# Sixteen expert slots with 3264 columns in place of 3287

## The chip, the core and the metric

The kernel runs on one core of one Trainium2 chip. The metric is the device time of one execution in microseconds (us). The kernel before took 423.11 us, the median of 6 runs that lay between 422.43 and 423.81 us.

A core has five engines that run side by side and wait for each other through semaphores: TensorE (PE; its weight loads are a row of their own, PEld), VectorE (DVE), ScalarE (ACT), GpSimd (POOL) and SyncE (SP), which here issues most of the DMAs. Matmul results land in PSUM and are copied from there by DVE or ACT into SBUF.

## The reference: what is computed

Two blocks, one after the other, in float32.

The first block is a recurrence (rwkv5) over 768 steps for 4 batches and 8 heads of 48 channels. Its output, seen as rows, is `x` with 3072 tokens of 384 values:

```python
cur = np.einsum('bhd,bhe->bhde', u[None] * kt, vt)
y[:, :, t] = np.einsum('bhd,bhde->bhe', rt, state + cur)
state = w[None, :, :, None] * state + np.einsum('bhd,bhe->bhde', kt, vt)
```

The second block sends each token to one expert of 16: to the best of 4 groups, and in that group to the best of 4 experts. Each expert is a two-layer network of 384 to 1024 to 384, and its result is scaled by the product of two softmax weights:

```python
g_idx = np.argmax(x @ w_group, axis=1)            # the group
e_idx = np.argmax(xg @ w_expert[g], axis=1)       # the expert in the group
h = np.maximum(xg[mask_e] @ w1[g, e], 0.0)
ye = h @ w2[g, e]
out[tok_idx] = combined[:, None] * ye
```

## The kernel before, in words

The kernel has two stages. In the first, 24 tiles of 128 tokens go through the recurrence in chunks, are routed, and their rows are scattered to a DRAM buffer `x_sorted`, which has a region for each expert. In the second, the experts are worked off one after the other.

How many tokens an expert gets is only known at run time, but each instruction has a fixed shape. So the kernel sorts the experts by their token counts on the chip and gives them *slots* of falling size. The list `SLOTS` (line 20) holds the sizes. The expert in slot `e` is computed with `SLOTS[e]` token columns, however few tokens it has; the columns that are left hold zeros, or rows whose index lies outside of the output. The first two experts are chosen early, after 16 of the 24 tiles (`pick_first`), the other 14 by the final counts. If an expert has more tokens than its slot (the comparison with `most`, lines 975 to 985 write the result to `left_i`), a slow path under `tc.If(more > 0)` (line 1039 on) handles the tokens that are left over, in further slots of 128 tokens, each with its own load of the weights.

The work of the second stage is a list of 17 items (`ITEMS`): the first slot of 256 is split in two items of 128 columns, and each other slot is an item of its own, of `SLOTS[e]` columns. An item of width w consists of:

- `columns` (L561, DVE): three transposes of the gathered rows `xg` into `xe`. They work on w rounded up to a multiple of 32 (`padded`).
- `up` (L596, PE): the first layer, in four calls (f = 0, 2, 4, 6). Each has 6 matmuls that move w columns, and ACT's ReLU to `hT` follows (L600). In the trace each matmul of float32 appears twice, so the four calls give 48 PE records.
- `w2_part` (L480, ACT): four copies of 128 x 768 that rearrange the second layer's weights; they don't depend on w.
- `down` (L617, PE): the second layer, in three calls (d = 0, 1, 2) of 8 matmuls that move w columns (48 records), each followed by ACT's copy to `yo` (L620).
- `pieces_out` (L649, L651, L656): DVE transposes and scales the result, on the padded width, and POOL scatters it to the output in pieces of 32 tokens. The last item goes another way (`turn_out`, `rows_out`, L634, L636, L669).

The order on PE and DVE is written out by hand (`manual_schedule`). For item i PE does `up(i, 0)`, `up(i, 2)`, `down(i-1, 1)`, `up(i, 4)`, `up(i, 6)`, `down(i-1, 2)`, `down(i, 0)`, then item i+1 begins. On DVE `pieces_out(i-1)` stands before `columns(i+1)`, so the transposes that item i+1 needs come after the last output work of item i-1.

Weights lie in two places used in turn: `w` (w1 and w2) and the memory of `kall` and `rall`, which the first stage has left. SP loads those of the expert after next as soon as `up(i, 6)` has read the last of w1 (L484 and L489), and it loads the rows of the item after next (L548, L554). PSUM gives 6 buffers (`bank`) in turn to all of these.

Of the kernel before, what the change touches and what calls it, by code (L numbers as in the profile page):

```python
# [16 lines left out]

SLOTS = [256, 240, 233, 222, 216, 212, 206, 202, 199, 196, 193, 190, 187, 184, 178, 173]  # L20
CAP = max(SLOTS)
FOUR = 4

# [11 lines left out]
def kernel(  # L35
# [30 lines left out]
    assert RING * 2 * H * D == KO * F and RING * 2 * H * DP >= FO * DM  # L66
    assert len(SLOTS) == GE == 16 and all(P < n <= 2 * P for n in SLOTS) and GE * (N + 1) < 2**20 and NCH > FOUR and FOUR * B * P >= GE * P
    assert DM % P == 0 and F % P == 0 and G == Eg == 4 and DM <= 512 and NT * GE <= 512
# [178 lines left out]

    for i, n in enumerate(SLOTS):
        nc.gpsimd.memset(most[:, i : i + 1], float(GE * n + GE - 1) + FIRST * max(2 - i, 0))
# [258 lines left out]

    ITEMS = [(0, 0, P), (0, P, SLOTS[0])] + [(e, 0, SLOTS[e]) for e in range(1, GE)]
    pools = {0: early}  # L510
# [528 lines left out]
    with tc.If(more > 0, preferred_fallthrough_block=False):  # L1039
        with tc.tile_pool(name="rest", bufs=1) as rest:  # L1040
# [7 lines left out]
            room = rest.tile([P, GE], FP32, name="room")  # L1048
            for i, n in enumerate(SLOTS):
                nc.vector.memset(room[:, i : i + 1], float(n))  # L1050
# [216 lines left out]
```

## Time and profile before

One execution was profiled. Its own time was 423.4 us, and the span from its first to its last instruction 421.6 us.

| What | Before |
|---|---|
| Median of 6 runs | 423.11 us |
| Profiled execution: time, span | 423.4 us, 421.6 us |
| PE busy | 406.3 us, 96% of the span |
| PE weight loads busy | 382.1 us, 91% |
| DVE busy | 183.2 us, 43% |
| ACT busy | 215.2 us, 51% |
| POOL busy | 202.2 us, 48% |
| HBM read, written | 70.15 MB, 16.44 MB |
| Granted TensorE clock, mean | 0.998 |

How to read what follows: a line of a profile names the line of the kernel (L617), the engine, the operation, and what it writes and reads (`po<-hT,w_parts`). `128*128 128x240` at a matmul means a stationary operand of 128 by 128 and a moving one of 128 rows by 240 columns. A line of the list in order of time begins with its start and its length in us; `x24` says that 24 instructions in a row were merged. Where an engine had to wait, the line ends in brackets with the length of the wait and what ended it. A line of busy time by stretch has the stretch (start and end in us), its length, and then for each of PE, PEld, DVE, ACT and POOL the busy time and, in brackets, the instructions; behind them stand the granted clock of PE, the busy share of the DMA engines and GB/s. The ends of matmuls are modelled, so that one of a row seems to overlap the next: what a matmul costs in a row of them is read from the starts.

### The profile page before, as it was taken

How to read it: one execution, taken by the hardware profiler on the slowest of the kernel's cores; microseconds unless marked ns; L12 is line 12 of the kernel's file. 1: busy time of each engine (PE TensorE's matmuls, PEld its weight loads, DVE VectorE, ACT ScalarE, POOL GpSimd, SP SyncE). 2: the span in 40 equal slices, each digit the busy share in tenths (PEclk: the TensorE clock that was granted, in tenths of full speed). 3: DMA queues.
4: the chain of work that ended last, by engine and by line, in shares of the span. 5: the costliest groups of instructions: out<-in, count | busy, mean ns of one | idle time of the engine just before them, and what ended most of it. 6: DMA issues, size and time to landing. Idle time of an engine off the chain costs nothing. (4 is left out here: it accounts for less than half of the span.)

```text
span 421.6 us, 9930 instructions
## 1 busy us (share of the span) xinstructions
PE 406.3 (96%) x3649; PEld 382.1 (91%) x3649; DVE 183.2 (43%) x620; ACT 215.2 (51%) x505; POOL 202.2 (48%) x214
## 2 busy tenths in 40 slices
PE   7799999999999989999999999999999999999993
PEld 6678888888887789999999999999999999999993
DVE  6566879787977834122130322304303403312211
ACT  2797777777776403551615426255255155256430
POOL 6875567777770733030624516336236246225453
PEclk9999999999999999999999999999999999999999
DMA  9999999991183959999987989789899899999001
GB/s 172 208 257 282 273 265 213 222 219 45 41 206 108 302 149 265 268 216 249 252 167 210 254 195 270 167 247 280 171 256 271 187 253 261 207 270 263 22 26 36
DMA packets 124476, 86.67 MB, mean 206 GB/s; under 512 B 96998, under 2 KB 113565, under 8 KB 124420
## 3 DMA queue, kind: packets, MB, share of 16 engines
q1 hardware_dynamic: 112732, 69.05, 72.5%
q0 software_dynamic: 4960, 9.48, 7.1%
q10 hardware_dynamic: 6728, 7.44, 5.2%
q8 instruction: 30, 0.49, 0.5%
q14 instruction: 26, 0.21, 0.2%
HBM read 70.15 MB, written 16.44 MB: 205 GB/s over the span
## 5 line engine op out<-in xcount | busy, mean ns | idle before, releaser
L656 POOL DMA_INDIRECT out_dram<-yp,ids x104 | 101.0, 972 | 160.2 <-DVE yo L611 124.7
L617 PE MATMUL po<-hT,w_parts 128*128 128x128 f32 (+15 forms) x816 | 139.4, 327 | 0.0
L617 PEld LDWEIGHTS po<-hT,w_parts 128*128 128x128 f32 x816 | 133.7, 190 | 0.9
L649 DVE STREAM_TRANSPOSE yr<-yo 128x224 f32<-128x224 f32 (+3 forms) x48 | 21.8, 460 | 181.9 <-ACT yo L620 181.3
L600 ACT ACTIVATE hT<-ph 128x256 f32<-128x256 f32 (+15 forms) x68 | 33.5, 492 | 79.8 <-PE ph L596 79.8
L596 PE MATMUL ph<-xe,w 128*128 128x128 f32 (+7 forms) x432 | 71.4, 322 | 1.3 <-DVE xe L561 1.3
L596 PEld LDWEIGHTS ph<-xe,w 128*128 128x128 f32 x432 | 68.5, 191 | 2.0 <-DVE xe L561 1.5
L596 PE MATMUL ph<-xe,kall 128*128 128x240 f32 (+7 forms) x384 | 68.5, 334 | 0.0
L596 PEld LDWEIGHTS ph<-xe,kall 128*128 128x128 f32 x384 | 65.4, 190 | 0.6
L705 ACT ACTIVATE am<-ident,du 128x128 f32<-128x128 f32 x192 | 58.7, 390 | 1.9 <-DVE du L697 1.5
L620 ACT COPY yo<-po 128x128 f32<-128x128 f32 (+15 forms) x51 | 16.2, 323 | 80.9 <-PE po L617 64.8
L735 DVE COPY_PREDICATED am<-later,pa 128x512 f32<-128x512 uint32 x48 | 32.7, 729 | 12.8 <-ACT yT L764 5.6
L480 ACT COPY w_parts<-rall 128x768 f32<-128x768 f32 x32 | 38.0, 1235 | 0.0
L480 ACT COPY w_parts<-w 128x768 f32<-128x768 f32 x29 | 34.4, 1234 | 0.0
L457 POOL DMA_INDIRECT x_sorted<-xt,place_i x24 | 23.8, 992 | 19.4 <-DVE rb L822 13.7
L691 POOL TENSOR_TENSOR dg<-rall,kall 128x768 f32<-128x768 f32 (+1 forms) x13 | 22.1, 1702 | 22.2 <-DVE du L697 21.3
L730 PE MATMUL pa<-rT,kT 48*128 48x128 f32 x384 | 28.8, 285 | 0.1
L758 PE MATMUL py<-am,vt 128*64 128x128 f32 x384 | 26.7, 280 | 0.0
L730 PEld LDWEIGHTS pa<-rT,kT 48*128 48x128 f32 x384 | 23.9, 187 | 2.2 <-issue 0.5
L684 POOL TENSOR_TENSOR kh<-kall,T 128x768 f32<-128x768 f32 (+1 forms) x12 | 21.6, 1804 | 8.5 <-DMA kall<-in_k_dram 5.9
L758 PEld LDWEIGHTS py<-am,vt 128*64 128x64 f32 x384 | 20.4, 136 | 4.7 <-issue 3.7
L720 ACT COPY kT<-pk 128x512 f32<-128x512 f32 x24 | 14.0, 583 | 20.4 <-PE pk L716 18.7
(146 smaller groups left out, 403.7 us busy)
## 6 DMA issues: line engine op xcount, KB each, us to landing
w<-in_moe_w_dram SPq DMA_DIRECT2D x32, 384.0 KB, 6.8
w<-in_moe_w_dram SPq DMA_DIRECT2D x8, 1536.0 KB
kall<-in_moe_w_dram SPq DMA_DIRECT2D x32, 384.0 KB, 8.0
rall<-in_moe_w_dram SPq DMA_DIRECT2D x8, 1536.0 KB, 12.6
x_sorted<-nothing ACTq DMA_DIRECT2D x4, 1544.0 KB, 8.1
rall<-in_r_dram SPq DMA_DIRECT2D x12, 384.0 KB, 7.1
vt<-in_v_dram SPq DMA_DIRECT2D x12, 384.0 KB, 7.2
kall<-in_k_dram SPq DMA_DIRECT2D x10, 384.0 KB, 6.0
```

The lines of the kernel that those rows point to most:

```text
L457: ins = nc.gpsimd.indirect_dma_start(out=xs_dram, out_offset=bass.IndirectOffsetOnAxis(ap=place_i[:, i : i + 1], axis=0), in_=xt[:, i, :], ...
L480: copy(w2_parts[e % 2][:, a : a + 2], w2[:, a : a + 2, :].rearrange("p f (c k) -> p f k c", k=KO))
L596: nc.tensor.matmul(ph[:, q, :], lhsT=w1[:, ko, P * (f + q) : P * (f + q + 1)], rhs=xe[:, ko, 0:w], start=(ko == 0), stop=(ko == KO - 1), s ...
L600: nc.scalar.activation(hTs[i][:, f : f + 2, 0:w], ph, AF.Relu)
L617: nc.tensor.matmul(po, lhsT=w2[:, fo, d, :], rhs=hT[:, fo, 0:w], start=(fo == 0), stop=(fo == FO - 1))
L649: nc.vector.transpose(yr[:, 0:b, :, d], y[:, d, 0:w].rearrange("p (b t) -> p b t", t=BL))
L656: ins = nc.gpsimd.indirect_dma_start(out=out_pieces, out_offset=bass.IndirectOffsetOnAxis(ap=ids[:, j : j + 1], axis=0), in_=yp[:, j], in_ ...
L691: engine.tensor_mul(dg, rts[g % RING][:, a0:a1, :, 0:D], kts[g % RING][:, a0:a1])
L705: nc.scalar.mul(am[:, e, hc, :], ident, dus[n // 2][:, n % 2, h : h + 1])
L730: nc.tensor.matmul(pa[e][:, hc, :], lhsT=kT[rows, hc, :], rhs=rT[rows, hc, :], start=True, stop=True, skip_group_check=True,)
L735: nc.vector.copy_predicated(am[:, e], earlier, pa[e])
L758: nc.tensor.matmul(py[e][DP * o : DP * (o + 1), j, :], lhsT=vt[:, a, 4 * o + 2 * j + e, :], rhs=am[:, e, 2 * o + j, :], start=(c == 0), st ...
```

## The change

The list of slot sizes gets new numbers; nothing else in the program differs. The old sizes add up to 3287 columns, the new ones to 3264.

```diff
-SLOTS = [256, 240, 233, 222, 216, 212, 206, 202, 199, 196, 193, 190, 187, 184, 178, 173]
+SLOTS = [256, 237, 233, 220, 214, 209, 205, 202, 199, 194, 193, 189, 185, 183, 176, 169]
```

Slot by slot the losses are 0, 3, 0, 2, 2, 3, 1, 0, 0, 2, 0, 1, 2, 1, 2 and 4 columns, 23 in all. The largest slot stays at 256 (`CAP`), which sizes the tiles and the zeroed part of each region, so no tile moves in memory. Every slot keeps its padded width (a multiple of 32), so all DMAs, the transposes of DVE and the scatters of POOL keep their shapes, but for the last item's second output tile, which has 41 rows in place of 45. The order of the instructions and their waits is the same on all five engines; what differs are the widths in L596, L600, L617 and L620, in the memsets that fill a result up to its padded width (L611), in the last item's row counts (L570, L574, L634, L636, L669) and the constants of `most`.

## The prediction

> **What bounds the kernel now.** I read the page first: which engine is busy, and where its idle time lies (in a group's line, behind the first bar the busy us and the mean ns of one, behind the second the idle us before them and what ended it).
>
> ```profile
> span 421.6 us, 9930 instructions
> PE 406.3 (96%) x3649; PEld 382.1 (91%) x3649; DVE 183.2 (43%) x620; ACT 215.2 (51%) x505; POOL 202.2 (48%) x214
> L617 PE MATMUL po<-hT,w_parts 128*128 128x128 f32 (+15 forms) x816 | 139.4, 327 | 0.0
> L596 PE MATMUL ph<-xe,w 128*128 128x128 f32 (+7 forms) x432 | 71.4, 322 | 1.3 <-DVE xe L561 1.3
> L596 PE MATMUL ph<-xe,kall 128*128 128x240 f32 (+7 forms) x384 | 68.5, 334 | 0.0
> ```
>
> PE is busy in 96% of the span, and the three groups of expert matmuls, 279 us together, had idle time before them once: 1.3 us at the start of the second stage (157.16 us), where no changed slot has begun. A busy share doesn't say that PE sets the end, so next came PE's waits from 185 us to the end; the answer is one line:
>
> ```profile
> PE pb L634 <- ACT yo L620: 0.4, 1, 0.4
> ```
>
> That is the last output tile. No expert matmul waited for a weight load from DRAM, a row gather, an eviction or a transpose. The busy time by stretch, cut where PE starts one item and the next (columns: PE, PEld, DVE, ACT, POOL), says it again:
>
> ```profile
> 157.16:162.62 5.46, 5.46 (x48) 5.46 (x49) 5.24 (x32) 1.15 (x3) 2.01 (x3) 1.00 0.79 226
> 189.00:406.90 217.90, 217.90 (x1289) 217.22 (x1288) 55.44 (x208) 96.31 (x147) 88.49 (x92) 1.00 0.87 216
> 218.31:235.99 17.68, 17.68 (x98) 17.68 (x97) 4.33 (x19) 7.46 (x11) 7.85 (x9) 1.00 0.86 213
> 365.48:380.52 15.04, 15.04 (x99) 15.04 (x97) 3.83 (x17) 7.17 (x11) 5.79 (x7) 1.00 0.98 251
> 380.52:395.16 14.64, 14.64 (x99) 14.64 (x97) 3.78 (x17) 7.16 (x11) 5.75 (x7) 1.00 0.63 177
> ```
>
> The reader is to see that PE's busy time equals the stretch in each, at full clock (1.00), and that items get shorter with their slots: 216 columns (the third line) take 17.68 us, 178 (the last) 14.64. ACT needs half of an item, DVE a quarter.
>
> **What a column costs.** From the first `up` of one item to that of the next lie 48 records of `up` and 16 of `down(i, 0)` at the item's own width and 32 of `down(i-1, 1)` and `down(i-1, 2)` at that of the item before. The 216 item (before it 222) is 64 x 216 + 32 x 222 = 20928 columns, the 178 item (before it 184) 64 x 178 + 32 x 184 = 17280. So a column costs (17.68 - 14.64) / (20928 - 17280) = 0.833 ns; 20928 x 0.833 ns is 17.44 us, and the other 0.24 us over 96 records are 2.5 ns for each. The 184 item checks it: 64 x 184 + 32 x 187 = 17760 columns, 14.80 + 0.24 = 15.04 us, as the fourth line has it.
>
> **Does it hold for the new widths?** Two ways in which it may not. First, weight loads: if these set the pace, narrower matmuls gain nothing. The first line above has 48 records of 128 columns, 113.8 ns each; whatever the floor is, it is no higher than that, and the narrowest new record, 169 columns, takes 169 x 0.833 + 2.5 = 143.3 ns. Second, odd widths: ten of the new slots are odd, five of the old ones. In order of time:
>
> ```profile
> 334.68 4.02 PE L596 MATMUL ph<-xe,kall 128*128 128x190 f32 x24
> 338.54 2.78 PE L617 MATMUL po<-hT,w_parts 128*128 128x193 f32 x16
> 350.20 3.96 PE L596 MATMUL ph<-xe,w 128*128 128x187 f32 x24
> 354.00 2.74 PE L617 MATMUL po<-hT,w_parts 128*128 128x190 f32 x16
> ```
>
> From start to start 24 records of 190 take 3.86 us and 24 of 187 take 3.80; the rate gives 3.860 and 3.800. An odd width costs nothing that this trace resolves (0.01 us in a run of 24). Five items turn from even to odd (237, 209, 205, 189, 183), each with 2 runs of `up` and 3 of `down`; at 0.01 us for each of these 25 runs it would be 0.25 us at most, in either direction.
>
> A rule is weighed here. The Trainium skill, "TensorE: Matmul & The Clock Gate", section "Back-to-back issue gap", gives for sustained pairs of weight load and matmul about 81 ns at 128 columns and 131 ns at 512, a slope of 0.13 ns a column. By that the saving below would be an estimated 0.29 us, which nobody could measure. Its formula for one matmul alone, N/2.4 + 2.5 ns, has the 2.5 ns of these rows but half their slope, and would give 0.92 us. The rows here are this kernel's own float32 records, and I take them.
>
> **The sum.** Removed: 23 columns (3, 2, 2, 3, 1, 2, 1, 2, 1, 2, 4 in the slots that change), each in 96 records of its item: 23 x 96 x 0.833 ns = 1.84 us, all on PE's gapless path. What else the change moves:
>
> - ACT's ReLUs and copies get shorter by under 1 ns a column (240 columns copied in 358 ns, 173 in 304). They hide beside PE, and what hides them is that ACT is idle for half of each item. ACT's four weight copies keep their length; they end some 4.8 us before `down` reads them (387.9 and 392.7 us in the 178 item).
> - DVE's memsets grow by up to 12 elements at 0.84 ns (78 ns for 24, 136 for 93): 10 ns, beside PE.
> - The tail after the last `down`, from 414.67 us to the end: one copy of 304 ns gets 3 ns shorter, and two DVE and one POOL instruction of 45 rows take 41. DVE's 45 rows took 540 ns against 572 for 128, so I cost this at zero.
> - DMAs keep sizes and order. SP's loads are released by PE (`up(i, 6)`), so they start earlier with it, and each deadline moves up by no more than an item and a half shrinks, 0.5 us. The tightest are those for the 233 item: w1 is issued until 167.0 us and there after at most 9.0, at 176.0, where PE wants it at 180.75; its rows until 161.6, there after at most 13.6, at 175.2, where DVE turns them at 179.1; its w2 at 167.4, and even with the 13.4 us of the longest w2 landing it is there at 180.8, where ACT copies it at 184.0. Later ones have more: for the 184 item, `kall` is issued until 347.2 and there after at most 8.5 us, at 355.7 for a use at 365.3. POOL scatters 6 to 8 pieces at 1.28 us a piece, 10.2 us of at least 14.6.
>
> So nothing is late next by these rows, except perhaps one wait, which is the closest thing in the trace. Before each item DVE writes `xe` only after it has scaled the item before last (`pieces_out(i-1)`), and PE covers this with `down(i, 0)`, which gets shorter, while DVE's padded widths don't:
>
> ```profile
> 393.77 0.76 DVE L651 TENSOR_TENSOR yp<-yr,gates 128x576 f32<-128x576 f32 x1
> 394.50 0.33 DVE L561 STREAM_TRANSPOSE xe<-xg 128x192 f32<-128x192 f32 x1
> 395.01 1.81 PEld L596 LDWEIGHTS ph<-xe,kall 128*128 128x128 f32 x12
> ```
>
> `xe` is there at 394.83 and PE's weight load begins at 395.01: 0.18 us. At no other item is it less. From ACT's last copy to PE's weight load for it took 0.06 us (414.70 + 0.30 to 415.06), so some 0.12 us are free. The change takes from it 16 records times the columns lost by the covering item: 2 columns here, 27 ns; 40 ns at most (3 columns), where 0.3 us are free. I take no wait. If none of this slack were usable, the 16 of 96 records of each item that cover it would gain nothing: 1.84 / 6 = 0.31 us lost. So the gain is 1.53 to 1.84 us for this term, and with the 0.25 us for odd widths 1.28 to 2.09.
>
> The profiled execution took 423.40 us (span 421.6 and 1.8 around it): 423.40 - 1.84 = 421.56. It stood 0.29 us above the median of 423.11, so the median is forecast at 421.27 us, 0.43% lower. About 0.2% (0.85 us) is what a measurement of this kernel can tell from no change; its six runs spread over 1.4 us.
>
> **Rivals.**
>
> 1. *The DVE chain takes it* (`xe` late at each item): 0.31 us lost, 421.6 us; still faster. For it: the slack falls to 0.18 us. Against it: 27 to 40 ns are taken.
> 2. *The experts are bound by data, and PE's lead is given back as waits for weights*: no change, about 423.1 us. For it: the DMA share is 0.86 to 0.99 from item to item. Against it: no PE wait on a DMA after 157 us, and the 3.2 us and more of slack above, which 1.8 us over the whole stage can't use up.
> 3. *A slot is too small* (the other side, slower): one expert with a token more than its slot sends the whole kernel through the slow path at L1039. Counting the reference's routing on its inputs, in slot order, gives 206, 211, 208, 207, 200, 200, 199, 198, 195, 193, 185, 185, 183, 170, 170 and 162 tokens. All fit; the tightest are 193 in 194 and 183 in 185 (before 193 in 196). It decides from two tokens more in that one expert, or three in the other. The nearest two candidates of any token differ by 2.8e-6 where the group logits spread by 0.01, so a rounding on the chip moves hardly one token. Price: a gather (at least 7.6 us), 96 records at 113.8 ns (10.9 us) and a scatter (6.2 us), 25 us at least; with its 16 zeroing stores in a row at 2.3 us, the shortest landing of a gather, and a weight load of 13.4 us, 75 us: 448 to 498 us.
> 4. *The narrower slots do nothing* (a pace set by weight loads): 423.1 us. Against it: 0.833 ns a column holds from 233 down to 173 columns.
>
> **How the numbers follow.** The forecast has 0.88, rival 1 0.06, rivals 2 and 4 together 0.04, rival 3 0.02. Rival 1 is also faster by over 0.2%, so faster has 0.94, same 0.04, slower 0.02. The time is the forecast's, 421.3. The range takes the gain of 1.28 to 2.09 us and 0.3 us more at both ends for where a median of few runs falls (as far as the profiled execution stood from it): 423.11 - 2.09 - 0.3 = 420.7 and 423.11 - 1.28 + 0.3 = 422.1.
>
> **What would show it.** The span falls to 419.75 us and PE's last `down` ends 1.84 us earlier, at 412.83. A stretch like the 216 item's (214 now, 220 before it) takes 64 x 214 + 32 x 220 = 20736 columns, 17.52 us. PE's waits after 185 us stay one line of 0.4 us; `xe` is ready 0.15 us or so ahead of PE at the last item. I am wrong if PE waits for `xe` or a DMA in the second stage, if the columns cost more at odd widths, or if lines of L1046 and later appear.

## The result: slower by 0.27%, and the profile after

The changed kernel took 424.24 us, the median of 17 runs (423.74 to 425.06), against 423.13 us for the kernel before (37 runs, 422.43 to 423.81). The ratio is 1.0027, with a 95% interval of 1.002 to 1.0033. The forecast was 421.3 us.

The profiled execution has a span of 423.1 us, 1.5 us more than before. The first question is whether the columns gave what they should. The busy time by stretch, first of the kernel before and then of the changed one, is cut at three places that both have: PE's first `up` of the second stage, PE's last two transposes, and POOL's last scatter (columns as before: stretch, length, then PE, PEld, DVE, ACT and POOL, the granted clock, the DMA share, GB/s).

```profile
157.16:415.06 257.90, 257.51 (x1540) 255.40 (x1540) 66.04 (x260) 112.50 (x172) 101.04 (x104) 1.00 0.87 214
415.06:417.37 2.31, 0.44 (x2) 0.18 (x2) 0.64 (x2) 0.00 (x0) 0.97 (x2) 1.00 0.04 11
417.37:421.60 4.23, 0.00 (x0) 0.00 (x0) 0.00 (x0) 0.00 (x0) 0.91 (x1) 0.78 0.19 67
```

```profile
157.41:413.47 256.06, 255.67 (x1540) 253.82 (x1541) 66.16 (x260) 112.25 (x172) 101.04 (x104) 1.00 0.87 216
413.47:415.78 2.31, 0.44 (x2) 0.18 (x2) 0.63 (x2) 0.00 (x0) 0.97 (x2) 1.00 0.04 11
415.78:423.10 7.32, 0.00 (x0) 0.00 (x0) 0.00 (x0) 0.00 (x0) 1.42 (x1) 0.63 0.13 39
```

The expert matmuls gained what was forecast: 257.90 - 256.06 = 1.84 us. The next stretch is the same. But from POOL's last scatter to the end it now takes 7.32 us where it took 4.23: 3.09 us more, over the 1.84 us that PE saved. (The second stage also began 0.25 us later. Nothing in the first stage was changed, and I don't explain that; in the profiled executions of the first four experiments below this start lay between 156.06 and 156.73 us, so it moves by more than that from one execution to the next.) The sum, -1.84 + 3.09 + 0.25, is the 1.5 us of the spans.

The last scatter is the one that writes the second output tile of the last item: 45 rows before, 41 now. The two scatters of L669 in order of time, before and after:

```profile
416.09 0.97 POOL L669 DMA_INDIRECT out_dram<-yt,ids  x1 [3.19 <-DVE yt L636]
417.37 0.91 POOL L669 DMA_INDIRECT out_dram<-yt,ids  x1 [0.30 <-POOLq L1039]
```

```profile
414.50 0.97 POOL L669 DMA_INDIRECT out_dram<-yt,ids  x1 [2.95 <-DVE yt L636]
415.78 1.42 POOL L669 DMA_INDIRECT out_dram<-yt,ids  x1 [0.30 <-POOLq L1039]
```

The first writes 128 rows and takes 0.97 us in both. The second has four rows less and takes POOL half a microsecond more. SP's wait for it at the end of the program, and the packets of POOL's DMA queue (the page's list of queues), again before and after:

```profile
SPq L1262 <- DMA out_dram<-yt,ids: 1.5, 1, 1.5
...
q0 software_dynamic: 4960, 9.48, 7.1%
```

```profile
SPq L1262 <- DMA out_dram<-yt,ids: 4.5, 1, 4.5
...
q0 software_dynamic: 5168, 9.48, 7.1%
```

The wait grew by 3.0 us, and the queue carries 208 packets more. That number is the clue. In the trace the rows of a tile leave in packets of up to three rows. 45 rows made 16 packets (besides 16 of 4 bytes, which both kernels have). 41 rows on one DMA engine make 14, and 14 on each of 16 engines are 224, which is 208 more than 16. By their sizes only 12 of the 224 hold rows of the output, and 12 of the 16 before; the others are 8 or 12 bytes long. So it looked as if 45 rows went to 15 engines with 3 rows each, and 41, a prime, to a single engine. The Trainium skill, "DMA: Bandwidth & Descriptors", section "Why a DMA increments its semaphore by 16 and not by 1", has such a rule: the number of engines is the largest up to 16 that divides the slowest dimension on both sides of the transfer. The page also has an exception on trn2, for some direct copies; the scatter here is an indirect one, and the runs have to tell. The experiments were made to see whether it is this that cost the time.

### The profile page after: what moved, and what is told of

Read it like the earlier page. It is cut to its first block, busy times and chain, and to the rows that moved or that the text cites. A ratio compares the mean times of both kernels' runs of the same rounds, so it can differ in the third digit from the quotient of the medians.

```text
span 423.1 us, 9930 instructions
## 1 busy us (share of the span) xinstructions
PE 405.1 (96%) x3649; PEld 381.0 (90%) x3649; DVE 183.3 (43%) x620; ACT 215.0 (51%) x505; POOL 202.5 (48%) x214
## 3 DMA queue, kind: packets, MB, share of 16 engines
q0 software_dynamic: 5168, 9.48, 7.1%
## 5 line engine op out<-in xcount | busy, mean ns | idle before, releaser
L617 PE MATMUL po<-hT,w_parts 128*128 128x128 f32 (+15 forms) x816 | 138.5, 326 | 0.0
L617 PEld LDWEIGHTS po<-hT,w_parts 128*128 128x128 f32 x816 | 133.0, 190 | 0.8
L600 ACT ACTIVATE hT<-ph 128x256 f32<-128x256 f32 (+15 forms) x68 | 33.5, 492 | 78.5 <-PE ph L596 78.5
L596 PE MATMUL ph<-xe,w 128*128 128x128 f32 (+7 forms) x432 | 71.1, 321 | 0.9 <-DVE xe L561 0.9
L596 PEld LDWEIGHTS ph<-xe,w 128*128 128x128 f32 x432 | 68.3, 191 | 1.5 <-DVE xe L561 1.0
L596 PE MATMUL ph<-xe,kall 128*128 128x237 f32 (+7 forms) x384 | 67.9, 333 | 0.0
L596 PEld LDWEIGHTS ph<-xe,kall 128*128 128x128 f32 x384 | 64.9, 190 | 0.5
L620 ACT COPY yo<-po 128x128 f32<-128x128 f32 (+15 forms) x51 | 16.2, 321 | 80.1 <-PE po L617 68.5
```

What stands on the lines that cost most here:

```text
L596: nc.tensor.matmul(ph[:, q, :], lhsT=w1[:, ko, P * (f + q) : P * (f + q + 1)], rhs=xe[:, ko, 0:w], start=(ko == 0), stop=(ko == KO - 1), s ...
L600: nc.scalar.activation(hTs[i][:, f : f + 2, 0:w], ph, AF.Relu)
L617: nc.tensor.matmul(po, lhsT=w2[:, fo, d, :], rhs=hT[:, fo, 0:w], start=(fo == 0), stop=(fo == FO - 1))
```

## The experiments

All ratios are to the kernel before, run beside it on the same chip.

### Which part of the change costs it

**Only the last slot changed.**

```diff
-SLOTS = [256, 240, ..., 184, 178, 173]
+SLOTS = [256, 240, ..., 184, 178, 169]
```

> Only the last slot changes, 173 to 169 columns, so that the last scatter has 41 rows in place of 45. Theory 'divisors' (a scatter of n rows is spread over as many DMA engines as the largest number up to 16 that divides n: 15 for 45 rows, 1 for 41): the matmuls gain 4 x 96 x 0.833 ns = 0.32 us, the tail loses some 3.0 us (what the tail of the changed kernel lost by its profile, less noise), so about 425.8 us against 423.1, ratio 1.006. Rival 'crowding' (the last scatter is late because the whole stage ends earlier while older output traffic is still under way): 0.32 us are too little for that, so 422.8 us, ratio 0.999.

Measured: 425.32 us against 423.08, ratio 1.0057 (1.0043 to 1.0071). The last slot alone, the smallest part of the change by work, makes the kernel 2.2 us slower. "Crowding" had 0.999.

**All slots changed but the last.**

```diff
-SLOTS = [256, 237, ..., 183, 176, 169]
+SLOTS = [256, 237, ..., 183, 176, 173]
```

> All the changed slots but the last, which keeps 173 columns and its scatter of 45 rows. Theory 'divisors': the gain of 19 columns, 19 x 96 x 0.833 ns = 1.52 us, comes through whole: 421.6 us, ratio 0.9964. Rival 'crowding': the stage ends 1.5 us earlier, so most of the loss stays: 424 us or more, ratio 1.002 and above.

Measured: 421.42 us, ratio 0.9966 (0.9956 to 0.9977). The gain of the 19 columns arrives, -1.7 us by the medians where 1.52 was worked out. So a stage that ends earlier does not by itself meet anything that holds it up, and "crowding" is out.

**The disputed cost by itself.** The kernel before, with none of its columns changed and four rows fewer in the last scatter:

```diff
             yt = out_rows[i][j][1]
+            m = n if j == 0 else 41
 ...
-                out=out, out_offset=bass.IndirectOffsetOnAxis(ap=ids[0:n, j : j + 1], axis=0), in_=yt[0:n],
+                out=out, out_offset=bass.IndirectOffsetOnAxis(ap=ids[0:m, j : j + 1], axis=0), in_=yt[0:m],
```

> The kernel before with one edit: the last scatter takes 41 of the 45 rows; the four rows left off belong to no token. No column changes. Theory 'divisors': the whole loss by itself, about 3.0 us: 426.1 us, ratio 1.007; the last scatter has over 200 packets more and lands some 3 us later. Rival 'narrow rows' (transposes, DVE and PE instructions on 41 partitions cost it): 423.1 us, ratio 1.000. Rival 'crowding': 423.1 us.

Measured: 425.87 us, ratio 1.0073 (1.0057 to 1.0089), 2.8 us slower. Its profile has the marks of the changed kernel (the scatter in order of time, SP's wait, the queue; the added line moves L669 to L670 and L1262 to L1263):

```profile
416.56 1.42 POOL L670 DMA_INDIRECT out_dram<-yt,ids  x1 [0.30 <-POOLq L1040]
...
SPq L1263 <- DMA out_dram<-yt,ids: 4.5, 1, 4.5
...
q0 software_dynamic: 5168, 9.48, 7.1%
```

PE, DVE and ACT still work on 45 rows here, so "narrow rows" is out too: the row count of this one DMA makes the loss by itself.

**All 23 columns saved, and 48 rows scattered.**

```diff
-        return [min(P, width(i) - a) for a in range(0, width(i), P)]
+        return [min(P, -(-(width(i) - a) // 16) * 16) for a in range(0, width(i), P)]
```

> The changed slots with all their columns, but the last output tile's rows are rounded up from 41 to 48, the next multiple of 16 (the added rows hold zeros and belong to no token). Theory 'divisors': 48 rows go over 16 engines, so the full 1.84 us of the 23 columns come through: 421.3 us, ratio 0.9957. Rival 'crowding': 424.2 us, ratio 1.0027.

Measured: 420.92 us, ratio 0.9948 (0.9933 to 0.9963). This version beats both kernels. The last scatter is back at 0.90 us, the final wait at 1.6 us and the queue at 4960 packets:

```profile
414.50 0.90 POOL L669 DMA_INDIRECT out_dram<-yt,ids  x1 [0.30 <-POOLq L1039]
...
SPq L1262 <- DMA out_dram<-yt,ids: 1.6, 1, 1.6
```

### Is it the divisor, or the size?

41 is not only prime but also less than 45. The same edit with other row counts, and the old slots with 48 rows, tell these apart. They ran on other chips, on which the kernel before took 433.3 us (the first four below) and 430.4 us (the last four), with a wider spread; so the ratios are coarser, and I also read the tail in the profile.

> The kernel before, its last scatter cut to 43 rows (the two rows left off belong to no token). Theory 'divisors': 43 is prime like 41, so one engine again: some 2.8 to 3.1 us lost, 426 us, ratio 1.007. Rival 'threshold' (the loss comes from some size below 45 on, in steps or in proportion): half of the 41-row loss or nothing, 423 to 424.5 us.

> The kernel before, its last scatter cut to 42 rows (the three rows left off belong to no token). It lies between 41 and 43. Theory 'divisors': 42 is 14 x 3, so 14 engines with 3 rows each, as 45 had 15: 423.1 us, ratio 1.000. Rival 'threshold': as slow as 43 or slower, 424 to 426 us.

> The kernel before, its last scatter cut to 38 rows (the seven rows left off belong to no token). Theory 'divisors': 38 is 2 x 19, so two engines with 19 rows each; the loss lies between that of one engine and none, and if it goes by the rows of one engine (19 against 41 and 3) it is 16/38 of some 2.8 us, 1.2 us: 424.3 us, ratio 1.003. Rival 'primes only' (any number that can be divided is spread well): 423.1 us, ratio 1.000. Rival 'threshold': more than at 41 rows, 426 us.

> The kernel before with its old slots and the last output tile rounded up from 45 to 48 rows. Theory 'divisors': 16 engines in place of 15, each 3 rows as before, so no change: 423.1 us, ratio 1.000 (0.998 to 1.001). It also tells whether the rounding by itself gave anything to the changed slots with 48 rows, which came out 0.3 us below the 1.84 us of its columns.

> The kernel before, its last scatter cut to 39 rows (the rows left off belong to no token, as in all of these). Theory 'divisors': 39 is 13 x 3, so 13 engines with 3 rows each and nothing lost: ratio 1.000. Rival 'threshold' (the fewer rows below 45, the worse): as slow as 41 rows, ratio 1.007.

> The kernel before, its last scatter cut to 37 rows, a prime. Theory 'divisors': all on one engine, 37 rows against 41, so nearly the loss of 41 rows, 2.7 us, ratio 1.006. Rival 'threshold' in its other direction (a loss only from 40 to 43 rows): ratio 1.000.

> The kernel before, its last scatter cut to 34 rows, all of which hold tokens: no padded row is left. Theory 'divisors': 2 x 17, so two engines with 17 rows each, a loss of 14/38 of 2.9 us over 3 rows for each engine, 1.1 us, ratio 1.0025. Rival 'primes only': ratio 1.000. If the loss came from the rows that hold no token, it would be none here either.

> The kernel before, its last scatter cut to 35 rows. Theory 'divisors': 7 x 5, so seven engines with 5 rows each in place of 3, a loss of 2/38 of 2.9 us, 0.15 us, which can't be told from none: ratio 1.000 to 1.001. It has one row more than the 34-row scatter and should be faster than it by 1 us.

Measured, sorted by the rows that one engine gets if the divisor decides. "Tail" runs from PE's last two transposes to the end of the span, in one profiled execution each.

| Rows | Engines x rows | Packets of POOL's queue | Last scatter on POOL, us | SP's last wait, us | Tail, us | Ratio (95%) |
|---|---|---|---|---|---|---|
| 48 (old slots) | 16 x 3 | 4960 | 0.90 | 2.1 | 7.05 | 0.9992 (0.9968 to 1.0016) |
| 45 (before) | 15 x 3 | 4960 | 0.91 | 1.5 | 6.54 | 1 |
| 42 | 14 x 3 | 4960 | 0.91 | 1.6 | 6.60 | 1.0015 (0.9991 to 1.0039) |
| 39 | 13 x 3 | 4960 | 0.92 | 2.0 | 7.06 | 1.000 (0.9984 to 1.0016) |
| 35 | 7 x 5 | 4976 | 0.94 | 1.6 | 6.62 | 1.0015 (0.9991 to 1.0039) |
| 34 | 2 x 17 | 5040 | 1.10 | 2.7 | 7.81 | 1.0018 (1.0004 to 1.0032) |
| 38 | 2 x 19 | 5056 | 1.13 | 2.7 | 7.74 | 1.0015 (0.9989 to 1.0041) |
| 37 | 1 x 37 | 5152 | 1.37 | 4.4 | 9.50 | 1.0067 (1.0044 to 1.0089) |
| 41 | 1 x 41 | 5168 | 1.42 | 4.5 | 9.65 | 1.0073 (1.0057 to 1.0089) |
| 43 | 1 x 43 | 5184 | 1.45 | 4.6 | 9.66 | 1.0080 (1.0053 to 1.0107) |

By size the rows would run 34, 35, 37, 38, 39, 41, 42, 43, 45, 48; no threshold can make 37, 41 and 43 slow and 39, 42 and 45 not. The three primes lose 2.6 to 3.3 us by their medians, and the numbers with 13 engines or more lose nothing that the ratios resolve. The packets fit exactly: 16 times the rows per engine divided by three and rounded up is 112 for 19 rows, and 112 - 16 = 96, the 96 packets that the 38-row scatter adds; for 43 it is 240 - 16 = 224, for 5 rows 32 - 16 = 16.

The two scatters on two engines are clear only in the profile: POOL's 1.10 and 1.13 us and a tail of 7.8 and 7.7 us lie between the groups. The tail is 1.2 us longer than with 45 rows, where 1.1 to 1.2 us were worked out, but the row counts that lose nothing spread from 6.5 to 7.1 us themselves. In time, 38 rows and 35 rows can't be told from none, and 34 rows (0.6 us by the medians, ratio above 1 by its interval) lose some half of what was expected, within the interval. The 35-row kernel came out 0.7 us faster than the 34-row one, where 1 us was worked out, but their intervals overlap. The 34 rows all hold tokens, so it isn't the padded rows that make the extra packets. The page's lines for POOL's queue, of 42, 38 and 37 rows in turn:

```profile
q0 software_dynamic: 4960, 9.48, 6.8%
```

```profile
q0 software_dynamic: 5056, 9.48, 6.9%
```

```profile
q0 software_dynamic: 5152, 9.48, 6.9%
```

The bytes stay at 9.48 MB while the packets grow: these extra packets carry almost nothing.

How the loss of 3 us divides can be read from the starts and ends of the packets. From POOL's start to the first packet with rows of the second tile it took 1.49 us with 45 rows (417.37 to 418.86) and 2.00 us with 41 (416.56 to 418.55, the kernel before with its scatter cut). That is 0.5 us more, as much as POOL's instruction got longer. From there on the 12 packets with rows need 0.40 us with 45 rows, many of them under way at once, and 3.02 us with 41 (to 421.57), none beginning before the one ahead of it has ended. The empty packets are over at 419.24, but for a few behind the last rows. The lines for POOL's queue (packets, MB, share of the time of 16 DMA engines), of the kernel before from 418.86 to 419.27, and with 41 rows from 418.55 to 419.27 and from 419.27 to 421.60:

```profile
q0 software_dynamic: 34, 0.06, 46.2%
```

```profile
q0 software_dynamic: 228, 0.02, 23.8%
...
q0 software_dynamic: 12, 0.04, 5.8%
```

In the last stretch, 2.3 us long, there are 9 packets with rows and 3 small ones, and 5.8% of 16 engines is about one engine (1/16 is 6.3%). So 2.6 of the 3.1 us are rows that leave in single file, and most of that passes when no empty packet is left to be worked off. The other row counts agree: the packets with rows take 3.0 us with 37 and 43 rows (one engine by the divisor), 1.4 and 1.5 us with 38 and 34 (two engines, two packets at a time), 0.5 us with 35 (seven). The kept trace doesn't name the engine of a packet; how many there were is read from these overlaps. Whether the empty packets also delay the first rows a little is not shown, and neither is what such a row count costs in a scatter that is not the last.

## Why the prediction was wrong

- *A column costs 96 x 0.833 ns, and 23 of them 1.84 us.* Right: 1.84 us between the same two places of PE's work. The stretch of the 214 item, for which 17.52 us were worked out, took that:

```profile
218.21:235.73 17.52, 17.52 (x98) 17.52 (x97) 4.35 (x19) 7.45 (x11) 7.84 (x9) 1.00 0.86 214
```

- *Odd widths and weight loads take nothing of it.* Right, since the whole 1.84 us came. The Trainium skill, "TensorE: Matmul & The Clock Gate", section "Back-to-back issue gap", has a sustained rule and a formula for a single matmul; what was estimated from their slopes (0.29 us and 0.92 us) was too small for these records, and the rows of the trace decided rightly.
- *No new wait on PE.* Right. From 185 us on its waits are still one line:

```profile
PE pb L634 <- ACT yo L620: 0.4, 1, 0.4
```

- *`xe` stays 0.15 us ahead at the last item.* Right: DVE has the first third of it done at 393.32 + 0.32 = 393.64 us, and PE's weight load begins at 393.80.

```profile
393.32 0.32 DVE L561 STREAM_TRANSPOSE xe<-xg 128x192 f32<-128x192 f32 x1
...
393.80 1.34 PEld L596 LDWEIGHTS ph<-xe,kall 128*128 128x128 f32 x9
```

- *The loads of weights and rows have slack.* Right: there is no PE wait on a DMA in the second stage.
- *The tail: "two DVE and one POOL instruction of 45 rows take 41. DVE's 45 rows took 540 ns against 572 for 128, so I cost this at zero."* This step is wrong, and the forecast fell with it. It measured +3.09 us in the profile and +2.8 us by itself on the chip, because 41 rows leave one packet after the other where those of 45 left side by side. I took the price of a POOL DMA from a DVE row, by the number of rows, and treated less as cheaper. The item below it, that DMAs keep sizes and order, left this one DMA out. The change touched one DMA in its shape, that DMA is the last work of the program with nothing behind which to hide, and I neither bounded it from the side of a loss nor looked up what decides how a scatter is spread.
- *The rivals.* None of the four named this. The one that ended slower, a slot too small, didn't happen: no instruction of the slow path is in the trace, and its 448 us are far off. The range, 420.7 to 422.1, was made from PE's uncertainties and the spread of the runs; the tail had no width in it. The signs of being wrong had the same gap: none of the three (PE waits, dearer odd widths, the slow path) came, and PE's last `down` ended at 413.08 us for a forecast 412.83, which is the 0.25 us of the later start. The span alone, 423.1 us for 419.75, showed the loss.
- *The forecast's size.* With 48 rows in the last scatter the kernel lands at 420.92 us, inside the range that was given for the change. The part of the sum that was worked out holds; the term that was set to zero was larger than all the rest.

## What to carry to other kernels

A size that is fitted to the data for one engine is also the shape of a DMA somewhere. Before a slot, a tile or a remainder is trimmed, look at every DMA whose row count follows from it. For the scatter here the good counts were a multiple of 16 (48) and those with a divisor from 13 to 16 (39, 42 and 45); 37, 41 and 43 were the dear ones, and 34 and 38, twice a prime, lay between. Padding 41 rows to 48 was worth some 3 us. And the last DMA of a program deserves a term of its own in any sum: here it had no cover, and what it lost was paid in full.

## What the runs showed of the hardware that I had not expected

A scatter by POOL of 41, 43 or 37 rows takes 1.37 to 1.45 us on POOL and keeps SP waiting 4.4 to 4.6 us at the end, one of 39, 42, 45 or 48 rows 0.90 to 0.92 us and 1.5 to 2.1 us. With 41 rows the packets are as many, and of such sizes, as if each of 16 DMA engines got 41 row entries, all but one engine's being empty: 5168 packets in the queue against 4960 for 45 rows, with the same 9.48 MB. The 12 packets with rows then follow one another for 3.0 us, where with 45 rows they overlap and take 0.4 us.
